# A fused convolution and SwiGLU kernel: the hand-written order of a steady pair drawn anew, more h sums on VectorE, output steps among the second pair's products

## The chip, the cores and the metric

The kernel runs on one core of a Trainium2 chip. The time is device microseconds (us) of one execution, as the median of several runs. Beside these there is one profiled execution, from which all views of the trace come.

## The reference

Two blocks stand one behind the other. A light convolution mixes each token with its six predecessors, with seven softmax weights per head; an RMS norm, a gate and a value product with a SiLU between them and an output product follow. All is float32.

```python
# x: (8, 4096, 192), weight: (8 heads, 7 taps)
w = softmax(weight, axis=-1)
y[b, s, h, g] = sum_k w[h, k] * x_pad[b, s + k, h, g]        # 192 = 8 heads x 24
x = y.reshape(32768, 192)
xn = x / sqrt(mean(x * x, axis=-1) + 1e-6) * rms_g
g, val = xn @ w_gate, xn @ w_val                             # 192 -> 1536
out = (g / (1 + exp(-g)) * val) @ w_out                      # 1536 -> 192
```

## The kernel before

**Pairs.** The 32768 tokens are cut into 32 pairs of two blocks of 512 tokens. Pair 0 is computed plainly. Pair 1 multiplies plainly but takes its output product in the fast form described below. Pairs 2 to 31 are the steady ones: all their matrix work goes by Strassen's scheme in Winograd's form, seven block products in place of eight, and the gate and value products run on operands that are split in three parts of few bits each, so that TensorE can take them in one pass each.

**One steady pair on TensorE.** The order is written out in `LINE`, 111 words. 69 of them are products (`Aa.2`, `P1.1`, `Q3.4` and so on; the number behind the point is one of six blocks of the 1536 columns). A product has six matmuls: three parts, each for gate and value on the two halves of the array (line 901). A cell (block, a to d) gathers several products in one of four double PSUM banks; `A..`, `P1` and `P5` open a cell, `f1` and `f5` open one by a copy or a sum. The other 42 words are output steps `oF.k`: form F of seven, block k of six. Forms 1, 6, 5 and 3 add into the accumulator X, 7 and 4 into Z, 2 into Y, which starts as a copy of X (`c1`). Their matmuls are line 928.

**What the other engines do in a pair.** A word of `ORDER` has the engine's letter first: A ScalarE, V VectorE, G GpSimd, S the DMA queue of SyncE.

- `g` and `m` (lines 978 and 985): SiLU of a cell's gate half into SBUF, then times the value half; `m` frees the cell's bank.
- `f1`, `f3`, `f4`, `f5` (lines 672 or 674, and 972): sums of cells in PSUM for blocks 1, 3 and 4.
- `h1` to `h4` (line 955): the sums of a block's four results that the output forms need. `o1.k` must have read the block before `h2.k` overwrites it, `o2.k` before `h4.k`; forms 5, 6, 7 and 3 read what h1, h2, h3 and h4 make.
- `c1`, `s7`, `c2`, `C22`, `C21` (672, 674, 1002): copies and sums of the accumulators. `c2` copies X before form 5 is added to it, `s7` copies Z before form 4, `C22` adds X to the copy of Z before form 3 is added to X, `C21` adds Z to the copy of X and frees Z's bank. `T11`, `T12`, `T21`, `T22` (943): transposes into the output tile, two instructions each; T11 frees Y's bank, T12 X's. `st` stores a part of the output (1034).
- For the next pair: `cv0` to `cv6` convolution taps (438, 442), `sq`, `red`, `pow`, `bc`, `mul` the norm (453 to 492), `pl` eight stores to a scratch in DRAM (1045), `ft` four loads of it in transposed form into xb (643), `x1` to `x4` sums of these tokens (829), `n`, `l`, `d` the three parts of each of five operands (672 or 674, 815, 817). n.0, n.1 and n.2 read three parts of xb, n.3 and n.4 the sums x1, x2 and x3, x4.
- For the pair after next: `ld`, eight loads of x into xh (151). They wait until the pl have read xh.

A `+` behind a word means the next pair, `++` the one after, `-` the one before; `p4` means that TensorE's program goes four words on. The text's order is the order of each engine's queue and settles who reads what; engines run ahead of each other as far as the semaphores let them. Banks go round in the order of the text: who opens a cell gets the bank that was given back first, those of X and Z ahead of others.

**The weight parts.** 45 pieces of split weights per pair come from DRAM (wd) through a ring of ten slots (line 787). When the last product that needs a piece has been issued, the load of the piece ten places further into that slot is put on SyncE's queue, behind which all that follows in that queue waits.

**The second pair.** `FIRST` is its order, the same words and, as W, the 60 steps that split the weights on the chip (`prepare`, lines 751 to 770) and store them to wd; R starts the ring, which lies over the place of pair 2's tokens.

## Time and profile before

| | us |
|---|---|
| runs of the kernel before | 2495.86, 2496.01, 2500.98; median 2496.01 |
| the profiled execution | 2502.22 |
| its span, first to last instruction | 2498.5 |
| one steady pair | 75.3 to 77.1 |
| TensorE busy in the span | 2466.9 (99%) |
| VectorE, GpSimd, ScalarE busy | 1998.1 (80%), 1099.6 (44%), 926.4 (37%) |

In the views, PE is TensorE's matmuls, PEld its weight loads, DVE VectorE, ACT ScalarE, POOL GpSimd and SPq SyncE's DMA queue. `x12420` is a count of instructions. What follows an arrow (`<-`) is what ended the idle time. A row of the windows has the stretch, its length, the busy time of PE, PEld, DVE, ACT and POOL, TensorE's granted clock, and the DMA engines' share and GB/s.

### The profile page before, as it was taken

The page shows a single profiled execution, that of the slowest core. Times are in us where ns is not written, and L with a number is a line of the kernel's source. Part 1 is how long each engine was busy: PE and PEld are TensorE (multiplying, and loading weights), DVE is VectorE, ACT ScalarE, POOL GpSimd, SP SyncE. Part 2 cuts the span into 40 slices and gives each one's busy share as a digit, 9 for nine tenths or more (in the row PEclk, how much of TensorE's full clock was granted, in tenths as well). Part 3 has the DMA queues.
Part 4 walks back from the last instruction along what each step waited for, and adds up shares of the span by engine and source line. Part 5 has one row for each costly group of instructions (what it writes and reads, how often), then busy time and mean ns, then how long its engine had stood idle before and what let it go on. Part 6 is the DMA issues. An engine that isn't in the chain of part 4 may idle for free.

```text
span 2498.5 us, 69292 instructions
## 1 busy us (share of the span) xinstructions
PE 2466.9 (99%) x29332; PEld 1963.2 (79%) x29332; DVE 1998.1 (80%) x2461; ACT 926.4 (37%) x1314; POOL 1099.6 (44%) x690
## 2 busy tenths in 40 slices
PE   8999999999999999999999999999999999999999
PEld 5546777787888788788778877878788778887787
DVE  8668878888778887787887787887788887788864
ACT  6342333432333433343333334333334333434322
POOL 0533453443544345444444444444544445544452
PEclk9999999999999999999999999999999999999999
DMA  7364676666676666776666776666766666766653
GB/s 150 60 190 111 154 193 188 154 175 157 163 200 174 160 164 163 175 198 159 173 164 158 188 193 153 174 160 159 200 191 148 169 162 167 201 175 164 161 151 101
DMA packets 703047, 412.25 MB, mean 165 GB/s; under 512 B 508891, under 2 KB 689043, under 8 KB 702739
## 3 DMA queue, kind: packets, MB, share of 16 engines
q1 hardware_dynamic: 698992, 406.92, 63.9%
q8 instruction: 231, 3.78, 0.6%
q10 hardware_dynamic: 3746, 0.92, 0.2%
q14 instruction: 78, 0.63, 0.1%
HBM read 349.26 MB, written 58.39 MB: 163 GB/s over the span
## 4 chain that ended last, share of the span: by engine, by line
PE 65%; DVE 12%; SPq 10%; DMA 9%; issue 2%; POOL 1%; ACT 0%; DVEq 0%; POOLq 0%; ACTq 0%
PE ps L901 53%; PE ps L928 10%; DMA xb<-xd 6%; SPq L151 5%; DVE part L817 3%; SPq L1034 3%; DVE y L442 2%; DVE o_sb L943 2%; PE ps L873 2%; DVE part L815 1%; DMA xh<-in_x_dram 1%; DMA out_dram<-o_sb 1%; SPq L643 1%; SPq L787 1%; DVE ht L955 1%
## 5 line engine op out<-in xcount | busy, mean ns | idle before, releaser
L901 PE MATMUL ps<-part,ring 64*128 64x512 f32 x12420 | 1436.2, 389 | 12.3 <-DVE o_sb L943 11.4
L901 PEld LDWEIGHTS ps<-part,ring 64*128 64x128 f32 x12420 | 1212.2, 184 | 229.6 <-DVE o_sb L943 24.5
L978 ACT ACTIVATE tt<-ps 128x512 f32<-128x512 f32 x744 | 441.8, 599 | 788.5 <-PE ps L901 730.2
L985 DVE TENSOR_TENSOR ht<-ps,tt 128x512 f32<-128x512 f32 x744 | 486.4, 686 | 243.3 <-ACT tt L978 239.1
L955 POOL TENSOR_TENSOR hs<-ht 128x512 f32<-128x512 f32 x150 | 247.3, 1657 | 592.8 <-DVE ht L985 592.8
L928 PE MATMUL ps<-ht,wo_sb 128*32 128x384 f32 (+2 forms) x7272 | 458.5, 381 | 6.6 <-DVE tt L1002 3.5
L928 PEld LDWEIGHTS ps<-ht,wo_sb 128*32 128x32 f32 x7272 | 331.2, 110 | 102.2 <-issue 15.4
L928 PE MATMUL ps<-ht,x 128*32 128x256 f32 (+2 forms) x6696 | 407.6, 380 | 0.0
L928 PEld LDWEIGHTS ps<-ht,x 128*32 128x32 f32 x6696 | 290.8, 110 | 90.0 <-issue 0.7
L955 POOL TENSOR_TENSOR ht<-ht 128x512 f32<-128x512 f32 x153 | 258.4, 1697 | 231.8 <-PE ps L928 227.1
L442 DVE SCALAR_TENSOR_TENSOR y<-xh,tp,y 128x1536 f32<-128x1536 f32 x186 | 350.6, 1885 | 3.2 <-ACT y L438 2.1
L972 DVE TENSOR_TENSOR ps<-ps,tt 128x1024 f32<-128x1024 f32 x180 | 221.9, 1233 | 25.0 <-ACT tt L672 10.7
L815 POOL TENSOR_TENSOR part<-tt,part 128x1024 fp32r<-128x1024 f32 x30 | 72.2, 2407 | 286.5 <-ACT part L672 286.5
L672 ACT CAST part<-xb 128x1024 fp32r<-128x1024 f32 x87 | 90.3, 1049 | 249.4 <-DMA xb<-xd 233.2
L672 ACT COPY tt<-ps 128x1024 f32<-128x1024 f32 (+1 forms) x152 | 121.8, 801 | 156.7 <-PE ps L928 147.4
L955 DVE TENSOR_TENSOR ht<-ht 128x512 f32<-128x512 f32 x219 | 157.6, 742 | 5.9 <-PE ps L928 5.8
L955 POOL TENSOR_TENSOR ht<-hs,ht 128x512 f32<-128x512 f32 x93 | 144.8, 1583 | 9.2 <-PE ps L928 9.2
L928 PE MATMUL ps<-hs,x 128*32 128x128 f32 (+2 forms) x2232 | 140.1, 379 | 0.0
L438 ACT ACTIVATE y<-xh,tp 128x1536 f32<-128x1536 f32 x29 | 45.8, 1580 | 233.0 <-DMA xh<-in_x_dram 225.3
L817 DVE SCALAR_TENSOR_TENSOR part<-part,xb 128x1024 fp32r<-128x1024 f32 x87 | 131.7, 1514 | 0.0
L928 PEld LDWEIGHTS ps<-hs,x 128*32 128x32 f32 x2232 | 98.6, 110 | 30.0
L672 ACT COPY ps<-ps 128x1024 f32<-128x1024 f32 x90 | 89.7, 997 | 71.4 <-PE ps L901 64.1
(135 smaller groups left out, 1520.5 us busy)
## 6 DMA issues: line engine op xcount, KB each, us to landing
ring<-wd SPq DMA_DIRECT2D x1350, 192.0 KB
xb<-xd SPq DMA_DIRECT2D x60, 512.0 KB
xd<-xh SPq DMA_DIRECT2D x240, 96.0 KB
xh<-in_x_dram SPq DMA_DIRECT2D x192, 105.0 KB
xb<-xd SPq DMA_DIRECT2D x60, 256.0 KB
out_dram<-o_sb SPq DMA_DIRECT2D x126, 96.0 KB
out_dram<-o_sb SPq DMA_DIRECT2D x62, 128.0 KB
wd<-part SPq DMA_DIRECT2D x5, 1152.0 KB
```

The source lines that it names most:

```text
L151: queue(eng).dma_start(out=dst, in_=src)
L442: nc.vector.scalar_tensor_tensor(out=y, in0=xk, scalar=w, in1=y, op0=ALU.mult, op1=ALU.add)
L672: nc.scalar.copy(out=dst, in_=src)
L815: e.tensor_tensor(out=split_of(g, 1).bitcast(F32R), in0=src, in1=high, op=ALU.subtract)
L817: nc.vector.scalar_tensor_tensor(out=split_of(g, 2).bitcast(F32R), in0=high, scalar=1.0 + SPLIT, in1=src, op0=ALU.mult, op1=ALU.subtract,)
L901: nc.tensor.matmul(out=self.both(j, c)[:, h, :], lhsT=left[HALF[h]], rhs=right[HALF[h]], start=(first and q == 0), stop=True, skip_group_c ...
L928: nc.tensor.matmul(out=self.acc(b)[i * Q : (i + 1) * Q, at : at + n], lhsT=left, rhs=cols, start=fresh, stop=True, skip_group_check=True, ...
L955: engine[eng].tensor_tensor(out=dst, in0=a, in1=b, op=op)
L972: nc.vector.tensor_tensor(out=self.both(j, c), in0=self.both(j, "b"), in1=s5, op=ALU.add)
L978: nc.scalar.activation(out=tt[:, t, :], in_=self.both(j, c)[:, 0, :], func=AF.Silu)
L985: nc.vector.tensor_tensor(out=self.hv(j, "abcd".index(c)), in0=self.both(j, c)[:, 1, :], in1=tt[:, t, :], op=ALU.mult,)
L1034: queue(eng).dma_start(out=to, in_=o[i * Q : i * Q + n, lo:hi, :])
```

## The change

Three things change.

1. `ORDER` and `LINE`, the steady order. The window's seam moves: the last nine output steps of a pair (`p9-`) now stand at the head of the next window, and C21, T22, T12 and T21 of that pair behind them. The products begin with block 0's c and d cells (`Ac.0 Ec.0 Ad.0`) where they began with `Aa.2`. Of the 24 h sums of a pair, 13 were on GpSimd; eleven of these go to VectorE (h1.0, h1.1, h1.3, h1.5, h2.1, h2.3, h2.4, h3.3, h3.4, h4.1, h4.3) and four others come to GpSimd (h2.2, h2.5, h3.2, h3.5), so that six stand there. c1 and n.3 go to ScalarE, f3.4 and l.2 to VectorE, x4 to GpSimd. c2 stands behind n.0, n.1 and n.3 in ScalarE's queue, where it stood behind n.0 and s7. SyncE's ld all stand beside the ft, ahead of the ring loads of the last six products.
2. `FIRST` and `PLAIN`, the second pair's: one form-1 output step follows each of the first five blocks' products, so X's bank is open from then on; all its h sums are on VectorE, where six were on GpSimd; c1 is on ScalarE.
3. `prepare`: three buffers for the weights' parts where there were two; the scratch behind them moves up.

The steady order, old and new, cut to the seam and the places that the text speaks of:

```diff
     ORDER = (
-        "p4 Vd.2 p1 Vd.3 Vcv1+ VT12- p4 Vcv2+ p2 Vcv3+ p1 Agd.0 Aga.2 An.4 Aga.0 Gl.4 Vmd.0",
...
-        "Agd.2 Vbc+ Vh3.0 Gmul+ Af3.4 Vmd.2 Spl.0+ p2 Spl.1+ Spl.2+ Spl.3+ Spl.4+ Vf4.4 p5",
-        "Sst0.0- Spl.5+ Spl.6+ Sst0.4- Aga.4 Gh1.3 Vh1.2 Vma.4 Vf5.4 Vh3.1 Spl.7+ Agb.5 Agc.4",
-        "Sld.0++ p3 Agd.4 Vh3.2 Vmb.5 Vmc.4 p1 Vmd.4 Sft.2+ Sft.0+ Sft.1+ Sst1.1- Sst1.2-",
-        "Sst0.1- Sft.3+ Sft.4+ p7 Agb.4 Agc.5 p1 Aga.5 Vmb.4 Vma.5 p4 Sft.5+ Sld.1++ p3 Vmc.5",
-        "Agd.5 Vmd.5 Vh2.0 Gh3.3 Gh1.4 Vc1 Gh3.4 An.0+ Gh1.5 Gh2.4 Gh2.3 Gh2.1 Vh3.5 Vh2.2",
-        "Vx1+ Vx2+ Vh2.5 p15 As7 Gh4.4 Ac2 p9 An.1+ An.2+ Sld.2++ Sld.3++ Sst1.0- Sst0.2-",
-        "Sld.4++ Sst0.3- Sst1.3- Sld.5++ Gh4.3 Gh4.1 Gx3+ Sld.6++ Sld.7++ Acv0++ Vh4.0 Vh4.2",
-        "Vx4+ Vn.3+ Vd.0+ Vl.0+ Vl.3+ Vh4.5 VC22 p4 Gl.2+ p6 Vd.1+ VT22 Vl.1+ VC21 p1 VT11",
-        "VT21",
+        "p9- Vd.3 Vcv1+ VC21- p1 VT22- VT12- Vl.1 Vcv2+ p11 Agd.0 Agc.0 An.4 VT21- Vmd.0",
...
+        "Agc.4 Vh3.0 Sst0.2- Sld.0++ Agd.4 Sst0.1- Sft.2+ Sft.3+ Sft.0+ Sft.1+ Sld.1++ Agb.4",
+        "Sld.2++ Sld.3++ Sft.4+ Gh3.2 Vmd.4 Vh1.1 Vmc.4 Vh3.3 Vmb.4 Sft.5+ Sst0.3- Sld.4++",
+        "Sld.5++ Sld.6++ Sst0.0- Sst1.1- Sld.7++ p7 Gh1.4 Aga.5 Agb.5 p1 Sst1.4- Agc.5 Vma.5",
+        "Vh3.4 p1 Vmb.5 Vh3.1 Vh1.5 p3 Sst1.3- Gh3.5 Vh2.3 p2 Vh2.0 Vmc.5 Vh2.4 Vh2.1 Ac1 p4",
+        "Gh2.2 Gh2.5 An.0+ p12 An.1+ Vd.0+ Vh4.2 Vx1+ Vh4.3 Vx2+ Vd.1+ An.3+ Ac2 Gx3+ Vl.3+",
+        "Vh4.5 p2 As7 Vh4.0 p6 An.2+ p2 Vl.2+ Gh4.4 Acv0++ Gx4+ Vl.0+ Vh4.1 VC22 VT11 Vd.2+",
     )
     LINE = (
-        "Aa.2 Ba.2 Ad.0 Aa.0 Bd.0 Ac.0 Ea.2 Ed.0 Ec.0 Ea.0 Ba.0 Bc.0 P1.1 Ab.2 P5.1 Bb.2 P6.1",
...
-        "o3.2 o4.3 o4.5 o4.1 o3.4 o3.3 o3.5 o3.0 o3.1",
+        "Ac.0 Ec.0 Ad.0 Ed.0 Bd.0 Aa.0 Bc.0 Aa.2 Ba.2 Ea.2 Ea.0 Ba.0 P1.1 P5.1 Ab.2 Eb.2 P6.1",
...
+        "Bc.5 o1.0 o1.4 o1.3 o1.5 o1.1 o1.2 o7.0 o7.1 o2.2 o6.3 o7.3 o7.4 o6.2 o6.0 o6.5 o2.3",
+        "o6.1 o7.2 o2.0 o7.5 o6.4 o2.5 o2.1 o5.5 o5.2 o5.4 o5.1 o5.0 o4.1 o2.4 o5.3 o4.5 o4.0",
+        "o3.3 o3.4 o3.2 o3.1 o4.2 o4.4 o4.3 o3.5 o3.0",
     )
```

The second pair, cut likewise, and the code:

```diff
-    PLAIN = tuple((j, c) for j in range(NP) for c in "abcd")
+    PLAIN = (
+        "a0 b0 c0 d0 o1.0 a1 b1 c1 d1 o1.1 a2 b2 c2 d2 o1.2 a3 b3 c3 d3 o1.3 a4 b4 c4 d4 o1.4",
+        "a5 b5 c5 d5",
+    )
     FIRST = (
...
-        "Agc.5 Vmc.5 p2 Agd.5 p1 Vmd.5 p1 Vh2.0 Vh1.5 p1 Gh2.4 p1 Vh2.2 Vh3.5 p1 Gh2.3 An.0+",
-        "p1 Gh2.1 p1 Vc1 Vh2.5 Vx1+ p2 Vx2+ Sld.1++ p1 Gh4.1 p1 Vh4.0 Sld.2++ p1 Vh4.2",
-        "Sld.3++ p2 Vx4+ p1 Vn.3+ p1 Vd.0+ Sld.4++ p1 Vl.0+ p2 As7 An.1+ Vd.1+ Vl.1+ An.2+",
-        "Vd.2+ Gl.2+ Gx3+ R Vl.3+ p1 Sld.5++ Gh4.4 p1 Sld.6++ p2 Ac2 Sld.7++ p2 Vh4.5 p4 VT11",
-        "Gh4.3 p3 Acv0++ VC22 p6 VC21 p4 VT22 VT21",
...
+        "Agd.5 p1 Vmd.5 p1 Ac1 Vh1.5 p2 Sld.4++ An.0+ Vh3.5 Vh2.5 p1 Vh4.2 Sld.5++ An.1+",
+        "Vl.1+ p1 Vd.0+ p1 Sld.6++ p2 Vx1+ p1 Gx3+ p1 Sld.7++ p1 Vh4.3 Vx2+ p1 Vd.1+ p1 An.3+",
+        "p1 Vh4.0 Vl.3+ p1 As7 p1 Ac2 An.2+ p1 Vh4.5 p1 Vh4.1 Vd.2+ Vl.0+ Vl.2+ Gx4+ R p2",
+        "Acv0++ p5 VT11 Vh4.4 p1 VC22 p1",
     )
...
-        st = room1[:, o % 2 * 3 * n : (o % 2 + 1) * 3 * n]
+        st = room1[:, o % 3 * 3 * n : (o % 3 + 1) * 3 * n]
         parts = st.rearrange("p (j q n) -> p q j n", j=NP, q=3)
         t1, t2, tmp, w4, e = (
-            room1[:, (6 + i) * n : (7 + i) * n].rearrange("p (j n) -> p j n", j=NP)
+            room1[:, (9 + i) * n : (10 + i) * n].rearrange("p (j n) -> p j n", j=NP)
             for i in range(5)
         )
...
             if self.p == 1:
-                for j, c in PLAIN:
+                first = [w for row in PLAIN for w in row.split()]
+                for w in first:
+                    if w[0] == "o":
+                        self.step(int(w[1]), int(w[3]))
+                        yield
+                        continue
+                    j, c = int(w[1]), w[0]
...
-                todo = [w for w in line_of if w[0][0] == "o"]
+                todo = [w for w in line_of if w[0][0] == "o" and ".".join(w) not in first]
```

37 rows, old and new, of tables (FIRST, LINE, ORDER) are left out of this document.

## The prediction

> **What bounds the kernel now.** I read the page first, then the table of windows, the waits, the timeline around one pair's start, and the chain of waits. The page's first part:
>
> ```profile
> PE 2466.9 (99%) x29332; PEld 1963.2 (79%) x29332; DVE 1998.1 (80%) x2461; ACT 926.4 (37%) x1314; POOL 1099.6 (44%) x690
> ```
>
> TensorE is busy for 2466.9 of 2498.5 us, so whatever this change does, it cannot take away more than some 30 us of idle time and what a lowered clock costs; the matrix work is untouched. The windows (us, then busy time of each engine, clock, DMA) show where the idle time is:
>
> ```profile
> 195.50:198.90 3.40, 3.40 (x40) 2.45 (x34) 3.35 (x5) 0.00 (x0) 1.27 (x1) 0.50 0.00 0
> 216.00:219.40 3.40, 3.02 (x30) 2.08 (x34) 0.33 (x1) 0.00 (x0) 0.00 (x0) 0.50 1.00 326
> 304.20:2422.00 2117.80, 2107.01 (x25704) 1718.45 (x25706) 1727.61 (x2071) 779.56 (x1063) 971.38 (x588) 1.00 0.67 171
> 304.20:379.50 75.30, 75.25 (x918) 59.42 (x918) 61.37 (x75) 27.85 (x38) 36.70 (x21) 1.00 0.69 173
> 758.90:836.00 77.10, 75.37 (x920) 62.86 (x920) 62.42 (x75) 27.92 (x38) 32.20 (x21) 1.00 0.67 169
> ```
>
> From 304.2 to 2422.0 run 28 steady pairs, 75.6 us each on average, the best 75.3 and the worst 77.1 with the same PE busy time: some pairs lose up to 1.8 us that others do not. The waits name the loser (engine line, what it waited for: us in total, times, longest):
>
> ```profile
> PEld ps L901 <- DVE o_sb L943: 24.5, 29, 2.2
> PE ps L901 <- DVE o_sb L943: 11.4, 16, 1.7
> PE ps L928 <- DVE tt L1002: 3.5, 1, 3.5
> PE ps L928 <- DVE ps L674: 2.3, 1, 2.3
> ACT part L672 <- DMA xb<-xd: 233.2, 31, 9.5
> ACT y L438 <- DMA xh<-in_x_dram: 225.3, 28, 17.6
> ```
>
> Nearly every pair (29 of 30), a product's weight load waits for a transpose of the pair before. The timeline around one such place:
>
> ```profile
> 1206.41 0.55 DVE L1002 TENSOR_TENSOR tt<-ps,tt 128x384 f32<-128x384 f32 x1
> 1206.88 0.63 DVE L943 STREAM_TRANSPOSE o_sb<-ps 128x256 f32<-128x256 f32 x2
> 1207.44 0.59 DVE L943 STREAM_TRANSPOSE o_sb<-tt 128x256 f32<-128x256 f32 x2
> 1207.96 1.86 DVE L817 SCALAR_TENSOR_TENSOR part<-part,xb 128x1024 fp32r<-128x1024 f32 x1
> 1209.20 3.74 PE L901 MATMUL ps<-part,ring 64*128 64x512 f32 x30
> 1209.75 1.21 DVE L817 SCALAR_TENSOR_TENSOR part<-part,tt 128x1024 fp32r<-128x1024 f32 x1
> 1210.88 1.80 DVE L442 SCALAR_TENSOR_TENSOR y<-xh,tp,y 128x1536 f32<-128x1536 f32 x1
> 1212.61 0.63 DVE L943 STREAM_TRANSPOSE o_sb<-ps 128x256 f32<-128x256 f32 x2
> 1213.30 44.15 PE L901 MATMUL ps<-part,ring 64*128 64x512 f32 x384 [0.37 <-DVE o_sb L943]
> ```
>
> The pair starts at 1209.20 with five products, then the sixth, Ac.0, needs the accumulator bank of X, which T12 (1212.61) frees only after d.2, d.3 and cv1. That d.2 took 1.86 us where its neighbour d.3 took 1.21: GpSimd worked on SBUF beside it. So the bound is PE's own rate plus one VectorE tail per pair.
>
> **The change, part by part.** (a) The boundary wait. The new order leaves nine output steps for the next window and turns X after them, and banks go round in text order: Ac.0 now takes Z's bank (freed by C21), Ad.0, two products later, X's (T12), Aa.0 a bank long free, Aa.2 Y's (T11). Its present price lies between 11.4 us (PE idle) and 24.5 (weight loads held); a load that is not held idles some 0.2 us anyway, 29 x 0.2 = 6, so I take 24.5 - 6 = 18 us as what can go. Whether it goes depends on VectorE's tail, which I follow from the landing of the next pair's tokens (xb), since the order puts three gates of PE behind it.
>
> Rates of PE, from the chain of waits (start, us, what):
>
> ```profile
> 1213.30 44.17 PE ps L901 x384
> 2089.45 27.44 PE ps L928 x337
> ```
>
> 64 products took 44.17 us, 0.69 each, so 69 take 47.6; the 42 output steps 27.44, 0.653 each. The landing and what follows it, from the timelines of SP, ACT and DVE:
>
> ```profile
> 1245.48 3.32 SPq L1045 DMA_DIRECT2D xd<-xh  x5
> 1252.38 0.53 SPq L1045 DMA_DIRECT2D xd<-xh  x1
> 1254.69 0.59 SPq L151 DMA_DIRECT2D xh<-in_x_dram  x1
> 1255.38 2.79 SPq L787 DMA_DIRECT2D ring<-wd  x3
> 1258.22 0.90 SPq L643 DMA_DIRECT2D xb<-xd  x2
> 1267.19 1.05 ACT L672 CAST part<-xb 128x1024 fp32r<-128x1024 f32 x1 [9.09 <-DMA xb<-xd]
> 1267.98 0.69 DVE L829 TENSOR_TENSOR tt<-tt,xb 128x512 f32<-128x512 f32 x1
> 1271.94 0.48 ACT L672 COPY tt<-ps 128x384 f32<-128x384 f32 x1 [2.12 <-PE ps L928]
> ```
>
> n.0, the first reader, starts at 1267.19, 58.0 us after the pair's first product; less this pair's boundary wait (about 0.7), 57.3 on a clock without waits. In SP's queue the fetches (L643) stand behind pl.7 (1252.38), ld.0, which waited 1.8 us for pl.7 to land, and three ring loads (2.79). The new text puts the ring loads into that wait, and two output stores, at some 0.6 us like ld.0, besides ld.0 ahead of the fetches: 1.8 - 1.2 = 0.6 us sooner. The steps before pl.0 (sq, red, pow, bc, mul) hang on the same products as now. So n.0 starts at 56.7 in a window like this one; its wait of 9.09 is longer than the mean (233.2/31 = 7.5), so 55.2 in a mean window. All eight ld (xh) now go out beside the fetches instead of behind the last ring loads; cv0's wait (225.3 us in all, on an engine with room) goes, and cv1 no longer stands behind it. The k=2 parts ft.4 and ft.5 stand behind three ld; only n.2, l.2 and d.2 need them, late.
>
> *Gate 1*, c2 on ScalarE, now behind n.3: X must be copied before the first form-5 step, the 24th output step, at 47.6 + 23 x 0.653 = 62.6. Chain from the landing, with durations from here and from the rows under (b): n.0 1.05, d.0 1.21, h4.2 0.74, x1 0.69, h4.3 0.74, x2 0.69, n.3 1.05, c2 0.48 = 6.65. That is 61.9 in the mean window and 63.4 in one like the quoted, 0.8 late; but VectorE starts an instruction before the last one's time is up (d.3 at 1209.75 for 1.21, cv1 at 1210.88), some 0.08 each, 0.4 in the chain: 0.4 late.
>
> *Gate 2*, C22 before the first form-3 step, at 47.6 + 33 x 0.653 = 69.1: after x2 (landing + 5.1) come d.1, l.3, h4.5, h4.0, l.2, l.0, h4.1, 7.2 us, then C22, 0.55: 68.1 or 69.6, against 69.1 or, behind a late gate 1, 69.5. In time, or late by 0.1.
>
> *Gate 3*, C21 by 75.0 and T12 by 76.4 (both 0.4 later behind a late gate 1): from 69.6 come T11 0.63, d.2 up to 1.86, d.3 1.21, cv1 1.80, C21 0.55 = 75.6, less 0.4 for the early starts, 75.2; T22 0.59, T12 0.63: 76.4. In time, by 0.2 to 1.7.
>
> (b) The engines' load. Rows:
>
> ```profile
> L955 DVE TENSOR_TENSOR ht<-ht 128x512 f32<-128x512 f32 x219 | 157.6, 742 | 5.9 <-PE ps L928 5.8
> L955 POOL TENSOR_TENSOR hs<-ht 128x512 f32<-128x512 f32 x150 | 247.3, 1657 | 592.8 <-DVE ht L985 592.8
> L815 DVE TENSOR_TENSOR part<-tt,part 128x1024 fp32r<-128x1024 f32 x30 | 37.5, 1249 | 0.0
> L815 POOL TENSOR_TENSOR part<-xb,part 128x1024 fp32r<-128x1024 f32 x29 | 95.8, 3304 | 0.0
> L972 DVE TENSOR_TENSOR ps<-ps,tt 128x1024 f32<-128x1024 f32 x180 | 221.9, 1233 | 25.0 <-ACT tt L672 10.7
> L674 DVE CAST part<-tt 128x1024 fp32r<-128x1024 f32 x30 | 27.0, 901 | 0.0
> L978 ACT ACTIVATE tt<-ps 128x512 f32<-128x512 f32 x744 | 441.8, 599 | 788.5 <-PE ps L901 730.2
> L985 DVE TENSOR_TENSOR ht<-ps,tt 128x512 f32<-128x512 f32 x744 | 486.4, 686 | 243.3 <-ACT tt L978 239.1
> ```
>
> Eleven h sums go from GpSimd to VectorE and four back, net 7 x 0.74 = 5.2 us; l.2 comes (1.25), f3.4 comes (1.2, by L972, the nearest that reads this shape from PSUM), n.3 (0.90), c1 (0.55, by L1002) and x4 (0.7) go. A steady pair has 1727.61/28 = 61.7 us of VectorE and 971.38/28 = 34.7 of GpSimd now; VectorE then has 61.7 + 5.2 + 1.25 + 1.2 - 2.15 = 67 of 75 us, GpSimd 34.7 less 7 x 1.66, less 3.3, plus 1.7 (x4, as an h sum) = 21.5. VectorE keeps 8 us of room and meets GpSimd less often. Between the products PE opens each bank behind a silu (0.60) and its product (0.69). The narrowest place I find is Ab.5, the 65th product, at 64 x 0.69 = 44.2: Q4.4 (the 59th) ends at 40.7, then gd.4 0.60, md.4 0.69, h1.1 0.74, mc.4 0.69: 43.4, in time by 0.8; a meeting on h1.1 would cost most of that.
>
> Here the Trainium skill speaks against the change: its page Perfetto Trace Analysis, section Optimizing Scalar/DVE Operations, would take work off a saturated VectorE, to ScalarE or even GpSimd. By that rule the boundary gain would be eaten: the second rival below. The same section warns that the two share a read port, so that moving between them may not help; the 1.86 beside 1.21 us above agrees.
>
> For the three gates and the narrow places I leave 8 us over 30 pairs: 0.4 in half of them by gate 1, and 2 us for the rest (bounds: 0, and 0.8 in each, 24).
>
> (c) The second pair. There c1 (L674) held PE 2.3 us and C22 (L1002) 3.5, and behind each stands a window of 3.4 us at half clock, 1.7 us each: 9.2 us in all. The new order runs o1.0 to o1.4 among the products, so the form-2 sums can start while PE multiplies, and c1 goes to an idle ScalarE: the first 4.0 us go. C22: 28 steps follow the last product, 18.3 us; VectorE has eight h sums, four l, three d, two x and T11 ahead of it, 5.4 + 5.0 + 3.6 + 1.4 + 0.6 = 16.0 us, plus 1.3 for the last silu and product and up to 2.2 for meetings: the wait is 0 to 1.7 us instead of 3.5. Against it, X holds one of four banks during the products. Three buffers for the weight parts (the third st) remove VectorE's waits for stores, which PE did not feel: nothing. I take -5 us, bounds -9 and 0. The skill's page TensorE: Matmul & The Clock Gate, section What's actually happening, has the clock fall after a whole idle window of about 3.4 us; by that, removing a 2.3 us wait would bring back no clock and the sum would be 1.7 us less. The row at 195.50 shows half clock behind just that wait, so the measurement decides.
>
> (d) The tail: T21 follows T12 at the very end, about +0.7 us before the last stores.
>
> Sum: -18 + 8 - 5 + 0.7 = -14 us. The profiled execution took 2502.22 us (3.7 around its span) and would take about 2488; the median of the runs is 2496.01, 6.2 lower, so **2482 us**.
>
> **The rivals.** *The landing does not come sooner (slower).* Gate 1 is the place: c2 queues behind n.3 on ScalarE, n.3 behind x2, x2 behind the landing. Should the ld and the stores cost the fetches what I credit, n.0 starts at 57.3 in every pair, c2 ends at 63.95 and PE stands 1.35 us: 30 x 1.35 = 40 against the 23 of (a) and (c), 2513. It decides from a mean start of n.0 of 56.7 (c2 late by 23/30 = 0.77 us). For it: before, c2 waited for PE (2.12) and nothing hung on n.3; now all of it hangs on one DMA. Against: the queue's order, and the mean wait of 7.5. *VectorE's load eats it (no change):* the gates miss by 0.6 in every pair, 18 us, leaving the second pair's gain less the tail: 2492. *All of it goes:* no gate misses and the second pair gives its 9: -26, 2470. *It does not do what it says* (the boundary wait stays where it is): only (c) and (d), 2492.
>
> **How the numbers follow.** About 0.2%, 5 us, is what a measurement of this kernel can tell from no change. Chances: the forecast 0.50, all of it 0.15, no change 0.12 (its two rivals together), slower 0.23. The range runs from the full gain, less 3 us for its last bound, to the slower rival short of its full price, which only pairs all alike would reach: 2467 to 2508. Faster 0.65, same 0.12, slower 0.23.
>
> **What would show it.** Right: the weight loads' wait for L943 falls below 8 us; pairs of 74.9 to 75.3 us, all alike; DVE busy near 67 us a pair and GpSimd near 21; n.0 starting 54 to 57 us after the first product; no half clock at the c1 place. Wrong: a PE wait for ACT tt L672 (gate 1) or DVE tt L1002 (gate 2) in most pairs, or waits at Ab.5 or P7.1.

## The result, and the profile after

The changed kernel takes **2478.18 us** (median of 4 runs, 2477.95 to 2478.9); the kernel before took 2498.49 beside it (4 runs, 2495.86 to 2503.44). The ratio is 0.9917 (95% interval 0.9899 to 0.9935): faster by 0.8%, by 20 us. The forecast was 2482, in a range of 2467 to 2508. Of the changed kernel the profiled execution took 2477.95 us, its span is 2476.2 (before 2498.5).

The page of before has this for the chain of work that ended last, by engine:

```profile
PE 65%; DVE 12%; SPq 10%; DMA 9%; issue 2%; POOL 1%; ACT 0%; DVEq 0%; POOLq 0%; ACTq 0%
```

The page of the changed kernel, busy time of each engine, then the chain that ended last:

```profile
PE 2458.6 (99%) x29332; PEld 1899.3 (77%) x29332; DVE 2123.7 (86%) x2646; ACT 936.8 (38%) x1345; POOL 610.5 (25%) x474
PE 93%; DVE 3%; SPq 2%; DMA 1%; issue 1%; POOL 0%; ACT 0%; DVEq 0%; POOLq 0%; ACTq 0%
```

Before, TensorE had 65% of the chain; now it has 93%. VectorE's busy time went up by 126 us (1998.1 to 2123.7) and GpSimd's down by 489 (1099.6 to 610.5). The windows, 28 steady pairs together, then two of them, the second the longest of all:

```profile
293.25:2394.20 2100.95, 2100.51 (x25707) 1661.47 (x25706) 1847.98 (x2239) 788.44 (x1091) 519.08 (x392) 1.00 0.66 173
1043.10:1118.15 75.05, 75.05 (x922) 59.45 (x920) 66.52 (x80) 28.23 (x39) 18.69 (x14) 1.00 0.67 173
1118.15:1193.56 75.41, 75.15 (x920) 59.05 (x918) 65.63 (x80) 28.13 (x39) 18.33 (x14) 1.00 0.67 172
```

A pair takes 2100.95/28 = 75.03 us, and TensorE is idle for 0.4 us in all 28 of them (before: 10.8). The waits that answer to those shown of before (engine line, what it waited for: us in total, times, longest):

```profile
ACT part L674 <- DMA xb<-xd: 78.5, 29, 4.4
ACT y L440 <- DMA xh<-in_x_dram: 50.9, 23, 3.6
...
PEld ps L909 <- ACT ps L674: 12.8, 62, 0.2
PEld ps L909 <- DVE ht L993: 8.1, 29, 0.4
...
PE ps L881 <- DVE ht L993: 1.5, 1, 1.5
...
PE ps L936 <- DVE tt L1010: 0.5, 1, 0.5
...
PE ps L936 <- ACT tt L674: 0.3, 1, 0.3
```

The wait of the products for the transposes (24.5 us on the weight loads, 11.4 on TensorE) is gone without a remainder. The waits for the copy c1 (2.3) and for C22 in the second pair (3.5, now 0.5) are gone too; one of 1.5 is new in its products (L881). ScalarE waits 78.5 us for the fetches where it waited 233.2. The boundary of one pair on VectorE, whose next pair starts its products at 1118.15:

```profile
1111.11 0.56 DVE L1010 TENSOR_TENSOR tt<-ps,tt 128x384 f32<-128x384 f32 x1 [1.51 <-PE ps L936]
1111.59 0.64 DVE L951 STREAM_TRANSPOSE o_sb<-ps 128x256 f32<-128x256 f32 x2
1112.15 1.96 DVE L819 SCALAR_TENSOR_TENSOR part<-part,xb 128x1024 fp32r<-128x1024 f32 x1
1114.03 1.21 DVE L819 SCALAR_TENSOR_TENSOR part<-part,tt 128x1024 fp32r<-128x1024 f32 x1
1115.16 1.80 DVE L444 SCALAR_TENSOR_TENSOR y<-xh,tp,y 128x1536 f32<-128x1536 f32 x1
1116.96 0.56 DVE L1010 TENSOR_TENSOR tt<-ps,tt 128x384 f32<-128x384 f32 x1
1117.44 0.63 DVE L951 STREAM_TRANSPOSE o_sb<-tt 128x256 f32<-128x256 f32 x2
1118.26 0.65 DVE L951 STREAM_TRANSPOSE o_sb<-ps 128x256 f32<-128x256 f32 x2 [0.20 <-PE ps L936]
```

C22 (the first row) waits 1.51 us for TensorE: VectorE is ahead. T12 (the last row) runs 0.1 us after the first product has started; before it ran at 3.4. d.2 (1112.15) takes 1.96 us in this place, beside GpSimd, as it took 1.86 in the other.

Put together for the profiled executions: the first product of the third pair starts at 218.19 where it started at 223.83 (-5.6); the 29 intervals between first products have a mean of 75.034 where it was 75.679 (-18.7); the last pair's end, from the last matmul to the end of the span, takes 7.03 where it took 5.09 (+1.9). The sum is -22.4, the spans differ by 22.3.

### The profile page after: what moved, and what is told of

Its sections match the earlier page's. It is cut to its first block, busy times and chain, and to the rows that moved or that the text cites. A ratio compares the mean times of both kernels' runs of the same rounds, so it can differ in the third digit from the quotient of the medians.

```text
span 2476.2 us, 69007 instructions
## 1 busy us (share of the span) xinstructions
PE 2458.6 (99%) x29332; PEld 1899.3 (77%) x29332; DVE 2123.7 (86%) x2646; ACT 936.8 (38%) x1345; POOL 610.5 (25%) x474
## 4 chain that ended last, share of the span: by engine, by line
PE 93%; DVE 3%; SPq 2%; DMA 1%; issue 1%; POOL 0%; ACT 0%; DVEq 0%; POOLq 0%; ACTq 0%
PE ps L909 57%; PE ps L936 34%; PE ps L881 2%; SPq L153 1%; SPq L237 0%; DVE ht L963 0%; DVE y L444 0%; DVE ht L1108 0%; SPq L1042 0%; DMA hs<-in_moe_w_out_dram 0%; DMA ht<-in_moe_w_gate_dram 0%; DMA x<-in_x_dram 0%; DVE part L344 0%; SPq L645 0%; DVE ht L993 0%
## 5 line engine op out<-in xcount | busy, mean ns | idle before, releaser
L909 PEld LDWEIGHTS ps<-part,ring 64*128 64x128 f32 x12420 | 1151.2, 184 | 271.1 <-ACT ps L674 12.8
L936 PE MATMUL ps<-ht,x 128*32 128x384 f32 (+2 forms) x6696 | 423.9, 379 | 0.0
L444 DVE SCALAR_TENSOR_TENSOR y<-xh,tp,y 128x1536 f32<-128x1536 f32 x186 | 338.3, 1819 | 0.2
L963 POOL TENSOR_TENSOR ht<-ht 128x512 f32<-128x512 f32 x90 | 115.8, 1287 | 554.7 <-DVE hs L963 234.0
L963 DVE TENSOR_TENSOR ht<-ht 128x512 f32<-128x512 f32 x282 | 193.3, 695 | 30.0 <-POOL hs L963 24.2
L674 ACT COPY ps<-ps 128x384 f32<-128x384 f32 (+1 forms) x121 | 104.1, 860 | 178.3 <-PE ps L936 104.3
L963 DVE TENSOR_TENSOR ht<-hs,ht 128x512 f32<-128x512 f32 x126 | 159.7, 1304 | 9.3 <-PE ps L936 8.7
L819 DVE SCALAR_TENSOR_TENSOR part<-part,xb 128x1024 fp32r<-128x1024 f32 x87 | 143.0, 1643 | 20.2 <-ACT part L674 20.1
L674 ACT CAST part<-xb 128x1024 fp32r<-128x1024 f32 x87 | 88.5, 1049 | 78.5 <-DMA xb<-xd 78.5
L963 DVE TENSOR_TENSOR hs<-ht 128x512 f32<-128x512 f32 x156 | 108.0, 693 | 0.2
L817 DVE TENSOR_TENSOR part<-xb,part 128x1024 fp32r<-128x1024 f32 x87 | 102.6, 1207 | 0.0
```

The costliest lines, as they stand in the source:

```text
L444: nc.vector.scalar_tensor_tensor(out=y, in0=xk, scalar=w, in1=y, op0=ALU.mult, op1=ALU.add)
L674: nc.scalar.copy(out=dst, in_=src)
L817: e.tensor_tensor(out=split_of(g, 1).bitcast(F32R), in0=src, in1=high, op=ALU.subtract)
L819: nc.vector.scalar_tensor_tensor(out=split_of(g, 2).bitcast(F32R), in0=high, scalar=1.0 + SPLIT, in1=src, op0=ALU.mult, op1=ALU.subtract,)
L909: nc.tensor.matmul(out=self.both(j, c)[:, h, :], lhsT=left[HALF[h]], rhs=right[HALF[h]], start=(first and q == 0), stop=True, skip_group_c ...
L936: nc.tensor.matmul(out=self.acc(b)[i * Q : (i + 1) * Q, at : at + n], lhsT=left, rhs=cols, start=fresh, stop=True, skip_group_check=True, ...
```

## The experiments

Ratios are to the kernel before, run beside each: 2500.34 us (2494.04 to 2509.77) for e1 to e4, 2500.43 (2494.96 to 2504.1) for e5 to e8, 2501.44 (2494.58 to 2508.17) for e9 to e11 and 2502.56 (2499.86 to 2509.21) for e12. "Pair" is the mean interval between the first products of the steady pairs in the profiled execution.

### The two halves of the change

**e1_steady**: the new ORDER and LINE, with FIRST, PLAIN, the second pair's order of output steps and the two buffers of before.

> The steady order after the change, with the second pair as it was before (its order, its output steps behind all products, two buffers). Theory: the steady pairs lose their wait at the boundary whatever the second pair does, so the mean pair is 75.0 us as in the changed kernel; the first product of pair 2 starts near 224 us as before, some 5.6 us later than in the changed kernel. Time: 2478 + 5.6 = about 2484. Rival, that the steady gain hangs on how the second pair hands over (its ring loads and its first tokens): pairs above 75.3 us and a time above 2488.

Measured: 2487.63 us (2484.74 to 2489.16), ratio 0.9939 (0.9918 to 0.9959). The pair is 75.13, and without its first interval (77.57) 75.04, as with the whole change. The first product of the third pair waits 3.6 us for C21 and starts at 225.68, 1.9 later than before; behind this wait the granted clock is 0.50 from 224.25 to 231.08, which is what makes the first interval long. The steady order alone brings the steady part of the gain.

**e2_second**: FIRST, PLAIN, the second pair's order of output steps and the buffers of after, with the steady order of before.

> The second pair after the change (its order, output steps among its products, three buffers), with the steady order as before. Theory: pairs stay at 75.3 to 77 us, and the first product of pair 2 starts near 218 us instead of 223.8: about 2493, some 5 us under the kernel before. Rival, that the second pair's part gives more than its 5.6 us, since pair 2 starts with less behind it: below 2488.

Measured: 2498.13 us (2491.46 to 2505.4), ratio 0.9993 (0.9977 to 1.0008). The first product of the third pair starts at 218.04, 5.8 sooner, but the pair takes 75.95 in this execution, 0.27 longer than in that of before, and 29 x 0.27 = 7.9 us eat it. The boundary waits are there as before (27.2 us on the weight loads); they differ from execution to execution by as much, so how much of the second half would last is not settled by this run. By the medians the two halves bring 12.7 and 2.2 us, the whole change 20.3; with the runs of e2 14 us apart, how far the halves help each other stays open.

### Why the boundary wait goes

**e3_turn_first**, on the kernel before:

```diff
-        "p4 Vd.2 p1 Vd.3 Vcv1+ VT12- p4 Vcv2+ p2 ...
+        "VT12- p4 Vd.2 p1 Vd.3 Vcv1+ p4 Vcv2+ p2 ...
```

> The kernel before with one word moved: T12 stands at the head of the window, ahead of d.2, d.3 and cv1, and nothing else is changed. Theory: the wait at the boundary is T12's place in VectorE's queue, so most of the steady gain is had by this word alone: pairs of 75.0 to 75.3 us, 2481 to 2486. Rival, that the sums moved from GpSimd to VectorE and the fewer meetings are what pays: d.2 is still slow and now later, the wait turns up at another gate of the same tail, and the time stays above 2492.

Measured: 2511.63 us (2508.5 to 2514.98), ratio 1.0043 (1.0025 to 1.0061): slower. The boundary of one pair, its first product at 1137.21, on VectorE:

```profile
1137.33 0.65 DVE L943 STREAM_TRANSPOSE o_sb<-ps 128x256 f32<-128x256 f32 x2 [1.62 <-PE ps L928]
1137.90 1.18 DVE L817 SCALAR_TENSOR_TENSOR part<-part,xb 128x1024 fp32r<-128x1024 f32 x1
1139.00 1.21 DVE L817 SCALAR_TENSOR_TENSOR part<-part,tt 128x1024 fp32r<-128x1024 f32 x1
1140.13 5.52 DVE L442 SCALAR_TENSOR_TENSOR y<-xh,tp,y 128x1536 f32<-128x1536 f32 x3
1145.57 2.47 DVE L985 TENSOR_TENSOR ht<-ps,tt 128x512 f32<-128x512 f32 x4
```

and on TensorE:

```profile
1146.31 4.07 PE L901 MATMUL ps<-part,ring 64*128 64x512 f32 x32 [0.65 <-DVE ht L985]
```

VectorE now stands idle for 1.62 us until the last matmul is done and T12 can run, and what comes behind is late: d.2 by 1.9 us, md.0 by 0.9 (8.4 us into the pair instead of 7.5). The wait has moved from the bank that T12 frees to those that the m's free, in 28 pairs. My theory fell: it is not T12's place alone.

**e4_rings_ahead**, on the changed kernel: two stores and ld.0 go ahead of the three weight loads, so that these stand straight ahead of the fetches, as before.

```diff
-        ... Sst0.4- Spl.5+ Spl.6+ Spl.7+ Vmd.5 p5",
-        "Agc.4 Vh3.0 Sst0.2- Sld.0++ Agd.4 Sst0.1- Sft.2+ Sft.3+ ...
+        ... Sst0.4- Spl.5+ Spl.6+ Spl.7+ Sst0.2- Sld.0++ Sst0.1- Vmd.5 p5",
+        "Agc.4 Vh3.0 Agd.4 Sft.2+ Sft.3+ ...
```

> The changed kernel with ld.0 and two output stores ahead of three ring loads in SyncE's queue where they stood behind them, so that the ring loads come straight ahead of the two large fetches, as before the change; the fetches keep their time within half a us. Theory: the ring loads' 576 KB still in the DMA rings are what made the landing late before; n.0 starts near 57 us after the first product instead of 54.9, c2 behind n.3 misses its time by 1 to 2 us in each pair, and PE waits for ACT tt at the first form-5 step: pairs of 76.0 to 77.0, 2510 to 2535. Rival, that the landing follows the time of the fetches' issue alone: n.0 near 55, pairs of 75.0, 2476 to 2481.

Measured: 2508.17 us (2502.5 to 2522.14), ratio 1.0026 (1.0008 to 1.0045): the whole gain and more is lost. Its waits:

```profile
ACT part L674 <- DMA xb<-xd: 138.3, 29, 7.4
...
PEld ps L936 <- ACT tt L674: 28.5, 22, 3.4
PE ps L936 <- ACT tt L674: 22.5, 19, 3.2
```

n.0 starts at 56.89 us into the pair instead of 54.90: 1.4 of the 2.0 us are time from the fetch's issue to n.0 (7.5 instead of 6.1), the rest is the issue itself (49.5 instead of 48.8). Gate 1 (form 5 behind c2, c2 behind n.3) holds the weight loads in 22 pairs and TensorE in 19. The wait for T12 does not come back.

**e5_load_between**, the mirror image, on the kernel before:

```diff
-        "Sld.0++ p3 Agd.4 Vh3.2 Vmb.5 Vmc.4 p1 Vmd.4 Sft.2+ Sft.0+ ...
+        "p3 Agd.4 Vh3.2 Vmb.5 Vmc.4 p1 Vmd.4 Sld.0++ Sft.2+ Sft.0+ ...
```

> The kernel before with one word moved: the first of the eight pieces of the input load (ld.0) goes behind the three weight loads of the steady pairs that now stand straight ahead of the fetches, so that the 3 us for which SyncE works on it lie between those loads and the fetches; nothing else changes. It is the mirror image of putting the weight loads straight ahead of the fetches in the changed kernel. Theory (a fetch lands late because the data of the weight loads is still queued ahead of it): the fetches are issued where they were (48.8 and 49.4 us in the pair), but n.0 starts at about 55.5 instead of 56.9; the wait of weight loads for L943 falls from 25 us to some 8, the pair from 75.68 to about 75.35, the time from about 2499 to about 2490. Rival (a): the landing follows the issue alone; n.0 stays at 56.9 and the time at 2499. Rival (b): n.0 is sooner, but the tail of VectorE (C21, T11, T21, d.2, d.3, cv1, T12) is late by itself; the wait for L943 stays above 20 us and the time within 3 us of the kernel before.

Measured: 2489.48 us (2488.3 to 2491.24), ratio 0.9958 (0.9944 to 0.9971), pair 75.30: one moved word brings 11 us. Its queue on SyncE in one pair, the first reader on ScalarE, and its boundary wait:

```profile
1170.52 1.51 SPq L787 DMA_DIRECT2D ring<-wd  x3
1172.23 0.75 SPq L155 DMA_DIRECT2D xh<-x  x1
1173.03 1.43 SPq L151 DMA_DIRECT2D xh<-in_x_dram  x2
1174.50 1.14 SPq L643 DMA_DIRECT2D xb<-xd  x2
```

```profile
1180.56 1.05 ACT L672 CAST part<-xb 128x1024 fp32r<-128x1024 f32 x1 [5.44 <-DMA xb<-xd]
```

```profile
PEld ps L901 <- DVE o_sb L943: 13.8, 28, 0.5
```

6.1 us pass from the fetch to n.0 here, 9.0 in the pair of before that the prediction shows. One thing differs from the expectation: the fetches themselves are issued 2.1 us sooner (at 46.7 instead of 48.8), because the weight loads now go out while ld.0 waits for the stores to scratch. n.0 is 3.7 sooner (53.2), which is more than I expected: 2.1 by the issue and some 1.6 by the shorter way from issue to reader. What is left of the wait is at most 0.5 in each pair.

**e10_swap**: e5, and T12 one place forward.

```diff
-        "p4 Vd.2 p1 Vd.3 Vcv1+ VT12- p4 Vcv2+ p2 ...
+        "p4 Vd.2 p1 Vd.3 VT12- Vcv1+ p4 Vcv2+ p2 ...
```

> e5_load_between (the kernel before with the load's first piece between the weight loads and the fetches; 2489.5, pair 75.30) with one more edit: T12 goes ahead of cv1 in VectorE's queue, in place of behind it. d.2 and d.3 stay ahead of T12, so that VectorE is still busy when the last matmul of the pair ends, and cv1 and T12 together end where they did. Theory (what is left at the boundary after e5 is the place of T12 alone, and VectorE only loses by an early T12 where it stands idle for it, as in e3_turn_first): T12 starts at 1.35 us instead of 3.07, cv2 still at 3.65 and md.0 at 7.2, the last 0.3 us of each boundary wait go, the pair is 74.95 to 75.0, the time 2480 to 2481: two moved words bring nearly what the whole new order brought. Rival: the wait turns up at the next bank that VectorE frees, as in e3_turn_first, and the time stays at 2488 to 2495.

Measured: 2480.74 us (2480.49 to 2481.84), ratio 0.9920 (0.9906 to 0.9935), pair 75.00. The boundary of one pair, whose first product starts at 1123.76:

```profile
1123.97 1.21 DVE L817 SCALAR_TENSOR_TENSOR part<-part,tt 128x1024 fp32r<-128x1024 f32 x1
1125.11 0.63 DVE L943 STREAM_TRANSPOSE o_sb<-ps 128x256 f32<-128x256 f32 x2
1125.67 5.48 DVE L442 SCALAR_TENSOR_TENSOR y<-xh,tp,y 128x1536 f32<-128x1536 f32 x3
```

T12 runs at 1.35, without an idle gap ahead of it, and the taps follow where they were. No wait for L943 is left. Two moved words in the old text make the steady pairs as short as the whole new order does. In the old order the sooner landing brings 11 us ((75.679 - 75.298) x 29) and T12's place 8.6 ((75.298 - 75.000) x 29), together 19.7, where the change brought 18.7. This is not a split of the change's own gain: in the new order a late landing costs 29 us at gate 1 (e4) and does not bring back the boundary wait. It does show that the eleven h sums moved to VectorE are not needed for pairs of 75.0 us; what they bring in the new order by themselves was not run.

**e8_copy_first**: e4 with c2 ahead of n.3.

```diff
-        "... Vx1+ Vh4.3 Vx2+ Vd.1+ An.3+ Ac2 Gx3+ Vl.3+",
+        "... Vx1+ Vh4.3 Vx2+ Vd.1+ Ac2 An.3+ Gx3+ Vl.3+",
```

> The changed kernel with the weight loads straight ahead of the fetches, as in e4_rings_ahead (2508), and besides with ScalarE's copy c2 ahead of n.3 instead of behind it. Theory (the 30 us that those loads cost all come through one gate: n.3 waits for the fetch, c2 stands behind n.3 in ScalarE's queue, and the first step of form 5 waits for c2): c2 starts at 61.3 us whatever the fetch does, the wait of L936 for L674 falls from 22.5 us to under 3, the pair from 76.05 to 75.05 and the time to about 2480. Rival: VectorE's own work behind the late n.0 (d.0, x2, d.1, l.3, h4) is late as well; the wait turns up at C22 or at the first product of the next pair, and the time stays above 2495.

Measured: 2519.81 us (2514.42 to 2535.52), ratio 1.0106 (1.007 to 1.0142). The wait at gate 1 is gone, and the next one takes its place, and more:

```profile
PEld ps L936 <- DVE tt L1010: 39.6, 30, 4.4
PE ps L936 <- DVE tt L1010: 31.5, 30, 4.1
```

n.0 is as late as in e4 (56.82), l.3 now waits for n.3, and C22 starts at 69.7 instead of 68.0, so that it ends behind the first form-3 step's time of 69.0. The rival was right: with a late landing all that VectorE does behind it is late, and gate 1 was only the first of two places where TensorE met it. In e4 the stop at gate 1 had hidden gate 2. A second cause adds to it. With TensorE no longer held, GpSimd's h4.4 starts at 67.4 and meets VectorE's late h4.1:

```profile
1122.21 1.41 POOL L963 TENSOR_TENSOR ht<-ht 128x512 f32<-128x512 f32 x1 [9.57 <-PE ps L936]
1122.39 1.77 DVE L963 TENSOR_TENSOR ht<-ht 128x512 f32<-128x512 f32 x1
```

h4.1 takes 1.73 us on average here and 0.69 in the changed kernel. That is 1.0 of the 1.7 us by which C22 is late, and as much as TensorE stands at it (31.5 us in 30 pairs); without the meeting C22 would, by this sum, nearly have been in time, which was not run.

### The second pair

**e6_c1_scalar** and **e9_c1_scalar**, on the kernel before: c1 in `FIRST` on ScalarE. In e6 it stands two steps too early, so that Y starts without the last of form 1's six steps; e9, whose edit is shown, has it at its old place.

```diff
-        "... Gh2.3 An.0+", "p1 Gh2.1 p1 Vc1 Vh2.5 Vx1+ ...
+        "... Gh2.3", "p1 Gh2.1 p1 Ac1 An.0+ Vh2.5 Vx1+ ...
```

> The kernel before with one edit in the second pair: the copy c1 is made by ScalarE ahead of its n.0 instead of by VectorE behind nine h sums. Theory (each wait of the second pair has its own cause): the 2.3 us wait of L928 for the copy and the stretch at half clock behind it go, the wait for C22 stays at 3.5, and the first product of the third pair starts about 4 us sooner, at 219.8 instead of 223.8. Rival: C22's time is set by VectorE alone, since the h sums and splits ahead of it are what is late; TensorE only comes sooner to the same wait, which grows from 3.5 to 6 or 7, and the first product still starts at 223 to 224. Then it was the h sums taken off GpSimd, with the steps moved ahead, that brought the 5.6 us of the change there.

> The kernel before with c1 of the second pair on ScalarE, at its old place in the order behind the sixth output step (in e6_c1_scalar it stood ahead of the last of the six steps that it sums up, so that it copied X without them). Theory, as e6 left it (TensorE and VectorE come sooner by c1, and give it back at the first steady boundary, where T12 stands in VectorE's queue behind cv1, which waits for ScalarE's cv0 and the input load): first product of the third pair at 216 to 219 in place of 223.8, the pair from there on 4 to 8 us longer than 75.7, the time within 3 us of the kernel before. Rival: what e6 won came of the steps that c1 left out; then the first product stands at 223 or later.

Measured: e6 2505.41 us (2493.55 to 2508.76), ratio 1.0015 (0.9999 to 1.0031); e9 2501.85 (2499.08 to 2512.7), ratio 1.0004 (0.9988 to 1.002). In both, the first product of the third pair starts some 8 us sooner (215.8 and 216.1), more than the whole change brought there, and the first steady interval takes 84.2 us instead of 75.7. The expectation of e6 had both sides wrong: not 4 us but 8, and then nothing. The rows of e9 on SyncE, ScalarE, VectorE and TensorE show where it goes:

```profile
210.87 4.60 SPq L787 DMA_DIRECT2D ring<-wd  x10
215.79 4.94 SPq L151 DMA_DIRECT2D xh<-in_x_dram  x3
```

```profile
223.10 1.57 ACT L438 ACTIVATE y<-xh,tp 128x1536 f32<-128x1536 f32 x1 [20.65 <-DMA xh<-in_x_dram]
```

```profile
224.71 1.82 DVE L442 SCALAR_TENSOR_TENSOR y<-xh,tp,y 128x1536 f32<-128x1536 f32 x1 [10.26 <-ACT y L438]
```

```profile
227.14 3.36 PE L901 MATMUL ps<-part,ring 64*128 64x512 f32 x14 [7.34 <-DVE o_sb L943]
```

The last three pieces of the input load stand behind the ring's ten first loads; cv0 waits for them, cv1 for cv0, T12 behind cv1, and the products for T12. In the changed kernel all eight pieces go ahead of the ring's start and cv0 runs at 205.26. So c1 off VectorE is worth nothing by itself in the whole time; that it and the loads ahead of the ring together make the 5.6 us of the change is what these rows suggest, and was not run alone.

**e7_two_buffers**: the changed kernel with two buffers for the weight parts (`o % 2`, scratch from 6).

> The changed kernel with the two buffers for weight parts of the kernel before in place of three. Theory (the third buffer hides nothing that was late): first product of the third pair at 218.2 as with three, time within 2 us of 2478. Rival: the parts of weights are prepared closer to the products now that five output steps stand among them, and with two buffers the preparation waits for the copies out of the buffer; VectorE, in whose queue the next part waits, holds up the products with it, and the first product starts 2 to 4 us later, the whole by as much.

Measured: 2480.27 us (2480.0 to 2480.54), ratio 0.9924 (0.9898 to 0.9951); first product at 218.58 (three buffers: 218.19), pair 75.09 (75.03). The third buffer is worth 0.4 us in the second pair, where it could act; the other 1.6 lie in steady pairs, which no buffer touches.

### A better version

**e11_best**, on the changed kernel: h3.0 and h2.0 of the second pair behind ma.1; the step o2.4 ahead of form 5; in the last pair form 4 ahead of form 3, and T21 ahead of T12.

```diff
-        ... p1 Gmul+ p1 Vh3.0 W Vh2.0", "p1 Aga.1 W W W Vma.1 p1 ...
+        ... p1 Gmul+ p1 W", "p1 Aga.1 W W W Vma.1 Vh3.0 Vh2.0 p1 ...
-        "... o2.5 o2.1 o5.5 o5.2 o5.4 o5.1 o5.0 o4.1 o2.4 o5.3 ...
+        "... o2.5 o2.1 o2.4 o5.5 o5.2 o5.4 o5.1 o5.0 o4.1 o5.3 ...
+                if self.p == PAIRS - 1:
+                    todo = line_of[:-9] + sorted(line_of[-9:], key=lambda w: w[0] == "o3")
-    for w in range(2, PAIRS + 1):
+    for w in range(2, PAIRS):
         run([w for row in ORDER for w in row.split()], w)
+    run("p3- VC21- VT22- VT21- p6- VT12-".split(), PAIRS)
```

> The changed kernel with four small edits. In the second pair h3.0 and h2.0 go behind ma.1, so that the meeting with GpSimd no longer delays the m's that free the bank: the 2.1 us wait there goes, first product of the third pair at 216.2. In the steady line the step o2.4 goes ahead of the first step of form 5: the copy c2 has 0.65 us more, the pair falls from 75.03 to 74.97 (1.6 us over 29 pairs). In the last pair the steps of form 4 go ahead of those of form 3, and T21 ahead of T12, so that only T12 and its stores are left behind the last matmul: from its end to the end of the span 5.1 us in place of 7.0. Sum: 2478.2 - 2 - 1.6 - 1.9 = about 2472.5. Rival for each: the moved h sums meet another GpSimd operation and the wait turns up at the next bank (first product stays at 218); the later steps of form 5 bring gate 2 closer (pair 75.03 or more); the ten stores set the end, not the transposes (7 us).

Measured: 2485.96 us (2483.86 to 2489.65), ratio 0.9941 (0.9927 to 0.9955): slower than the changed kernel. Two of the three parts did what was expected: first product at 216.52, end 5.05. The pair took 75.45, and the weight loads waited 14.1 us for C22. The groups of the changed kernel, line engine operation, count, busy time and mean ns of one:

```profile
L817 DVE TENSOR_TENSOR part<-xb,part 128x1024 fp32r<-128x1024 f32 x87 | 102.6, 1207 | 0.0
...
L831 POOL TENSOR_TENSOR tt<-xb,tt 128x512 f32<-128x512 f32 x29 | 37.2, 1282 | 0.0
```

and of e11:

```profile
L817 DVE TENSOR_TENSOR part<-xb,part 128x1024 fp32r<-128x1024 f32 x87 | 157.0, 1830 | 0.0
...
L831 POOL TENSOR_TENSOR tt<-xb,tt 128x512 f32<-128x512 f32 x29 | 63.6, 2193 | 0.0
```

GpSimd's h4.4 overwrites what o2.4 reads. With o2.4 moved it starts 3.9 us sooner, at 63.5 us into the pair, x4 behind it at 64.8, and both run beside VectorE's l.2 and l.0: those take 2.19 and 2.11 us on average instead of 1.22, x4 takes 2.19 instead of 1.28, and C22 starts at 68.9 instead of 68.0. One such meeting, h4.4 and x4 on GpSimd, l.2 and l.0 on VectorE:

```profile
1109.34 1.29 POOL L965 TENSOR_TENSOR ht<-ht 128x512 f32<-128x512 f32 x1 [6.89 <-PE ps L938]
1109.40 2.31 DVE L817 TENSOR_TENSOR part<-xb,part 128x1024 fp32r<-128x1024 f32 x1
1110.59 2.26 POOL L831 TENSOR_TENSOR tt<-xb,tt 128x512 f32<-128x512 f32 x1
1111.63 2.30 DVE L817 TENSOR_TENSOR part<-xb,part 128x1024 fp32r<-128x1024 f32 x1
```

These rows look like turns and not like a common slowing: h4.4, which came first, takes its usual 1.29, and each of the others ends 1.1 us after the one before it on the other engine has ended (1110.63, 1111.71, 1112.85, 1113.93).

**e12_best**: e11 with o2.4 where it was.

> e11_best without the moved step o2.4: the changed kernel with h3.0 and h2.0 behind ma.1 in the second pair, and in the last pair the steps of form 4 ahead of form 3 and T21 ahead of T12. Theory (in e11 the moved step let GpSimd's h4.4 and x4 start at 63.5 and 64.8 us instead of 67.4 and 68.6, beside VectorE's l.2 and l.0, which took 2.18 and 2.09 us instead of 1.22 each, so that C22 was 0.9 us late): with o2.4 back, l.2 and l.0 take 1.22, C22 starts at 68.0, the pair is 75.03; first product of the third pair at 216.5, last matmul to end 5.05: 2478.2 - 1.7 - 2.0 = about 2474.5. Rival: l.2 and l.0 are slow because of the other edits (the pair stays at 75.4, the time at 2486).

Measured: **2474.53 us** (2473.65 to 2474.8), ratio to before 0.9882 (0.9865 to 0.99). First product at 216.84, pair 75.026, end 5.02; l back at 1206 ns. It beats the changed kernel by 3.6 us, in the two places where the prediction had seen a price for the change.

## Why the prediction was right, and where it was not

- **What bounds the kernel** (the boundary wait, by T12's place behind the late work of VectorE): right. The wait is gone, and e5 and e10 take it away by its two parts.
- **The landing, "0.6 us sooner" by SyncE's queue**: the step that failed. The fetches are issued at 48.8 us, just where they were: the two stores and ld.0 took all the room that was credited. n.0 nevertheless starts at 54.90 (55.2 forecast), because only 6.1 us pass from the issue to it, not 8.1. That the figure came out is luck: by the working, n.0 of before lies at 55.8 in a mean window without waits. The trace has 56.85, or some 56.2 without the boundary wait of 0.6. So the working started 0.4 too early, and credited 0.6 where 1.3 were gained. In six kernels the time from the fetch to n.0 falls with the gap between the last weight load and the fetch (the gap is from issue to issue; means over 29 pairs):

| kernel | gap, us | fetch to n.0, us |
|---|---|---|
| before | 0.5 | 8.1 |
| e3_turn_first | 0.5 | 8.2 |
| e4_rings_ahead | 0.5 | 7.5 |
| e10_swap | 1.7 | 6.6 |
| e5_load_between | 1.7 | 6.6 |
| after | 3.4 | 6.1 |

  Weight loads of 192 KB issued just ahead delay the fetch by 1.4 to 2 us. The prediction looked at when the fetch is issued, and not at what is in front of it. That the gap decides is shown by e4, where little else moves; e5 agrees, though its fetches are also issued sooner. The DMA packets of the traces show the mechanism (a weight load goes in packets of 1536 bytes, a large fetch in packets of 4096): of the 576 KB of the three weight loads, some 520 KB have still to move when the fetch is issued in before and in e4, 180 in e5, and 4 in after, and the fetches' last packet ends 6.6, 6.5, 5.9 and 5.3 us after the issue.
- **Gates 1 to 3**: the chains behind the landing were right in length, but they are not what sets the times in the changed kernel. In e4, with its late landing, c2 ends 6.3 us after n.0 starts (6.65 less 0.4 forecast). In the changed kernel c2 waits for TensorE in 22 of 28 pairs and ends at 62.04 on average (61.9 forecast) against the first form-5 step at 62.48; VectorE is ready for C22 at 66.7 and waits in all 28, for the last form-5 step, so that C22 starts at 68.0 and ends at 68.6 (an end at 68.1 was forecast) against the first form-3 step at 69.0; T12 waits for TensorE as well and ends 0.8 us into the next pair (1.4 forecast for a late window). The working followed VectorE alone and left out that c2 and C22 read what TensorE has just added up, so that at either gate no more than some 0.5 us are left however soon the tokens land. That the ends lie so close to the forecast is chance.
- **The slower rival**: e4 and e8 show that both gates bind when n.0 is 2 us late. The rival's place and point of decision (n.0 at 56.7; e4 has 56.9, 2508) were right, and only its condition did not come true. It priced 40 us for n.0 at 57.3; e4 shows (76.05 - 75.03) x 29 = 29 at 56.9.
- **"I leave 8 us" for the gates and narrow places**: over-sized. The mean pair stands 0.084 us above the best (75.034 against 74.95), 2.4 us in all. So the steady pairs gave 18.7 us where -18 + 8 allowed 10.
- **Loads of the engines**: 1847.98/28 = 66.0 us of VectorE a pair (67 forecast), 519.08/28 = 18.5 of GpSimd (21.5). What was left on GpSimd got quicker as well: its h sums took 1657, 1697 and 1583 ns by their three forms (hs<-ht, ht<-ht, ht<-hs,ht) and take 1290, 1287 and 1529.
- **The second pair**, -5: measured -5.6. The c1 wait is gone and C22's is 0.5, as in the working. "X holds one of four banks" was the right worry: the new 1.5 us wait in the products stands there. That the gain lasts only with the input load ahead of the ring's start was not in the working; e9 showed it.
- **The tail**, +0.7: mis-sized, +1.94. I counted T21 and not that all ten stores now start behind the last matmul; e12 takes it back.
- **From the profiled execution to the median**: I took off 6.2 us, the distance between the two before. The changed kernel has no such distance (2477.95 and 2478.18), and its runs lie within 1 us where they lay within 7.6. Those of e10, without the boundary wait either, lie within 1.4, which suggests that this wait is what made the executions of before differ. The sum itself was 8 short (-14 against -22.3), and the 3.7 us around the span were 1.8; these two made the forecast too long by 10, the 6.2 made it too short, and they partly cancelled: 2482 against 2478.
- **"VectorE's load eats it"**, the rival by the section Optimizing Scalar/DVE Operations of the Trainium skill's page Perfetto Trace Analysis: did not come true. By that rule a saturated VectorE should be relieved; here work came to it (80% to 86% busy), and it still had 1.3 us of room at C22. That the kernel is faster is not the moved sums' doing as far as is shown: e10 has the same pairs without them. The section's warning of the shared port agrees with e11 (1.22 to 2.19 us on VectorE, 1.28 to 2.19 on GpSimd).

## What to carry to other kernels

A DMA's landing hung here on what was issued just ahead of it in its queue: before reordering engines, look at the gap between a large load and the transfer that the critical chain waits for, and fill it with something small. When an instruction that frees a resource is moved forward, put it behind as much work as keeps its engine busy until its input is there (e10), not at the head of the queue (e3). A copy that reads an accumulator cannot come sooner than the last step into it: look for that bound beside the chain on the copying engine. A wait that goes can have hidden the next one, and an earlier start on an idle engine can cost its neighbour: price both before moving anything.

## What the runs showed of the hardware that was not expected

- VectorE and GpSimd hold each other up in sums with two inputs in SBUF: 1.22 to 2.19 us for 128x1024, 1.28 to 2.19 for 128x512 on GpSimd (e11). By the rows of e11 and e8 the one that comes first runs at its own pace or nearly so, and the other ends later by about what was left of the first. The Trainium skill's page SBUF — State Buffer, section Who interferes with whom, has a VectorE instruction with two SBUF inputs contend with a GpSimd instruction that reads SBUF; these rows agree. A tap on VectorE (128x1536) has a mean of 1.82 us in after and 1.89 in before.
- TensorE's clock fell to half behind the 2.3 us wait for c1 in the profiled execution of before, but not behind the same wait in e1, e3, e5 and e10; behind the 3.5 us wait for C22 it fell in all five, for 3.4 us or 6.8. So the 1.7 us that the prediction took for the first stretch came in one execution of five. The windows ahead of two such places, in before and in e2, and one of e8 behind which the clock did not fall:

```profile
192.20:195.50 3.30, 0.99 (x24) 0.65 (x21) 3.30 (x5) 0.00 (x0) 1.42 (x1) 1.00 0.00 0
1514.60:1518.00 3.40, 1.52 (x16) 1.24 (x16) 3.40 (x4) 0.00 (x0) 0.00 (x0) 1.00 0.02 5
2348.70:2352.10 3.40, 0.03 (x2) 0.00 (x0) 3.40 (x4) 1.58 (x1) 2.37 (x2) 1.00 0.70 208
```

  TensorE was busy for 0.99 of 3.30 us and for 1.52 of 3.40 (a wait of 1.9 us), and the clock fell all the same, to 0.50 for 3.4 us; in e8 it was busy for 0.03 of 3.40 us, and the clock stayed at 1.00. The length of the wait alone does not decide. The Trainium skill's page TensorE: Matmul & The Clock Gate, section What's actually happening, has a window of about 3.4 us that runs free of the kernel; that fits with one wait having the effect in one execution and not in the next. That the window must be wholly idle does not fit with the first two rows.
